# Split stores of three output tiles and another order of steps in a fused linear-attention and gated-MLP kernel

## The chip, the cores and the metric

The kernel runs on one core of a Trainium2 chip. The metric is the device time of one execution, in microseconds, measured on the chip. A core has TensorE (PE) for matmuls, VectorE (DVE), ScalarE (ACT) and GpSimd (POOL) for elementwise work, and SyncE (SP), which issues this kernel's DMA transfers between HBM and the on-chip memory SBUF. Matmuls write to PSUM.

## The reference

The kernel adds two branches and a residual. S = 2048 tokens, D = 512, H = 32 heads of 16, F = 1792. Inputs are bf16. `B_x` is not used: both branches work on `A_x`.

```python
x   = A_x
xn  = layernorm(x)
# branch A: linear attention with a "hedgehog" feature map
q, k, v = split(xn @ wqkv)                     # per head, 16 wide
phi(t)  = concat(softmax(t @ w_phi), softmax(-t @ w_phi))   # 32 features per head
kv  = phi(k)^T @ v ;  z = sum over tokens of phi(k)
A   = ((phi(q) @ kv) / (phi(q) . z + 1e-6)) @ wo
# branch B: gated MLP without a nonlinearity
B   = ((xn @ w_gate) * (xn @ w_up)) @ w_down
out = x + A + B
```

## The kernel before

The 2048 tokens are 16 tiles of 128, in four groups of four. The program is a long prologue written in place (loads, the first tiles' layer norm, the first value projections) and then a list of named steps. Each step is a small function in a dictionary `steps`, and the string `ORDER` (from line 25 on) names all of them in the order in which they are issued. The suffix `/v`, `/g` or `/a` runs an elementwise step on DVE, POOL or ACT. A second table, `SLOTS`, says which buffer of a ring each new tile takes: the PSUM banks (`s`), working tiles (`x`), feature maps (`phi`), transposed attention outputs (`oT`), output tiles (`o`) and so on. Nothing reorders the steps afterwards: each engine, SP too, runs its own instructions in the order of the list, and an instruction waits for its inputs, for its buffer to come free, and for all that is ahead of it on its engine.

The names that matter, with the line that does the work. A number behind a name is a tile or a weight block:

- `g`, `u`, `gc`, `h`: gate and up matmuls of one 128-column block of F for 512 tokens (line 333), the copy of the gate to SBUF (339 and 341) and the product (353). Tokens 0 to 1023 go this way.
- `fk`, `fq`: matmuls that fold `w_phi` into the k and q weights (455). `s`, `sc`, `a`, `xt`: layer norm of tiles 4 to 15, and the DMA transpose of the result (507).
- `vk`, `k`, `q`: projections (319). `x` and `y` behind k or q: the two exponentials on ACT (521); `r` and `i`: sums and their reciprocals on DVE (533, 538); `kp`, `qp`: the normalised features on POOL (543).
- `kv`, `kvm`: the sum of phi(k)^T v over all tiles (574) and its masked copy (579); `vc` copies the values to SBUF. `qt`: DMA transpose of phi(q) (600). `ab`: phi(q) against kv in PSUM (611); `de`, `rd`, `ot`: denominator, reciprocal, quotient (622 to 639); `oT`: DMA transpose of the quotient (645).
- `f`, `fs`, `fo`: the down projection and `wo` of one token tile (663), its sum with x (673, 676) and its store (680). `F` is the last quarter of tile 12's columns.
- `p`, `k`, `j`, `m`, `d4`: for tokens 1024 to 2047 the gate and up products are taken by a scheme with seven half-size matmul products in place of eight, for 7 pairs of blocks of F (797). It needs sums of tokens `z` (774) and of weights `up`, `t` (758), copies `k` of products (339, 341), joins `j` on DVE (812, 816) and products `m` of gate and up (819).
- `P`, `K`, `A`, `B`, `J`, `X`: the down projection of six of the last eight tiles, taken as the pairs (9, 13), (10, 14) and (11, 15), uses the same scheme. It needs sums `S` of the hidden values (894) and copies and differences of the down weights `cb`, `ct`, `wt` (874). `P2a.9` is the first part of product 2 of pair 9 (matmuls at 924), `P2w.9` the attention part of tile 9 through `wo`. Products stay in PSUM or are copied by `K` (341), `A` and `B` add to the copy (947), and `J` joins on DVE into one half, 256 columns, of an output tile `o_sb` (953). `J2` and `J3` fill the two halves of the earlier tile of the pair, `J4` (columns 0 to 255) and `J8` (256 to 511) those of the later one. `X` stores a finished tile (979).

Two rules are added by the code that walks the list. When a DVE step reads and writes only SBUF (`both_in_sbuf`: names `z`, `t`, `wt`, `cb`, `ct`, `S`, `m`, `A`, `B`, `a`, `ws` with a number), the next POOL instruction of the list waits for it. When a PSUM phase begins (`=k`, `=ab`, `=f`, `=ab2`), two banks change hands.

The walk and the store, word for word:

```python
    for word in ORDER.split():
        name, _, eng = word.partition("/")
        fn, default = steps.pop(name)
        ...
        if on_pool and turn is not None:
            tc.add_manual_dep(on_pool[0], turn.name, AFTER, reason="turns")
            turn = None
        if on_dve and both_in_sbuf.match(name):
            turn = on_dve[-1]
...
        for t in (n, m):
            steps[f"X{t}"] = (lambda t=t: nc.sync.dma_start(out=out_view(t, t + 1)[:, 0, :], in_=mine["o", t][:]), None)
```

Of the kernel before, what the change touches and what calls it, by code (L numbers as in the profile page):

```python
# [20 lines left out]
def _bcast_ap(ap_in: bass.AP, new_ap):  # L21
# [1 line left out]


ORDER = """
g2 gc2/v u0 g3 gc3/a u2 h2 g1 u1 gc1/v h1 fk2 g0 gc0/v u3 fka2/a h3 h0 fk0 fkv0/v g8 g4 fkv2/a fka0/a k0 gc8/v
s7 u8 h8 s5 s6 s4 gc4/a n1.1 ky0 k1 n0.1 n0.3 kx0 ky1 kr0 ki0 g10 g7 gc10/a sc4 a6/g k3 u4 u6 h4 gc7/a xt6 g9 g6
u10 s8 s11 a7/v n1.6 kx1 a4/a u7 gc6/a g13 xt7 n0.0 ky3 xt4 h10 u13 h6 u9 gc13/a gc9/a a5/a xt5 h7 kr1 s14 ki1
h9 n1.4 g12 gc12/v kp0/g =k k2 u12 u5 g5 h12 s10 h13 n0.5 kx3 n0.2 kx2 n1.5 ky2 s9 sc8 a9/g u14 g14 gc14/a gc5/v
h5 kp1/g a8/g xt9 g15 g20 kv0 h14 wq n0.4 u20 g18 gc15/a n1.2 n0.6 gc18/a gc20/a s13 kr3 s12 s15 kr2 u18 vk5.0  # L30
vk5.1 ky5 vc5/a h20 g16 gc16/v h18 ki3 g24 vk4.0 vk4.1 u16 ki2 kx5 n1.0 n2.3 kr5 gc24/a u15 kv1 vc4/a sc12 a13/g
kp3/g kp2/g vk6.0 g19 h16 h15 vk6.1 gc19/v kx4 ky4 n1.3 fq2 wr0 ki5 a10/v wf0 vc6/v u19 kv2 kx6 fqv2/a ky6 g21
fq0 xt10 fqv0/a g23 gc23/a fqa2/v h19 gc21/a kr6 kr4 ki4 a15/g g17 u21 u24 a12/a xt12 xt15 kv3 h24 wp0 kp5/g xt8
ki6 h21 kp4/g ws0 up00/v kp6/g u23 a14/a xt14 fqa0/a gc17/a vk7.0 vk7.1 kx7 ky7 vc7/v kr7 h23 up01/g vk9.0 kv4
g26 gc26/a kv5 vk9.1 a11/a t00/g kx9 ky9 kr9 ki7 u26 up21/a vk8.0 vk10.0 h26 vc9/v vk8.1 kx8 ky8 kr8 vk10.1 u17
h17 kp7/g t01/g up30/a vc10/a ki9 kp9/g kx10 t03/g g11 ky10 q0.0 q0.1 g25 gc25/a gc11/a vc8/v xt11 xt13 kr10
t02/v ki8 ki10 u11 u27 h11 kv6 vk12.0 g27 gc27/v h27 kv7 qx0 n2.5 kp8/g kp10/g qy0 n2.2 qr0 vk12.1 qi0 u25 h25
qp0/g qt0 ky12 kx12 up40/a kr12 vk11.0 vk11.1 ki12 vc12/a kv8 ky11 kx11 vc11/a kr11 kp12/g ki11 vk13.0 vk13.1
ky13 kx13 kr13 ki13 q1.0 g22 q1.1 kv9 u22 vk14.0 kv10 vk14.1 qy1 gc22/a qx1 h22 up20/a kp11/g vk15.0 q4.0 kp13/g
vk15.1 qr1 ky14 kx14 qi1 qp1/g vc14/a kx15 ky15 kv11 q4.1 q5.0 kr14 ki14 vc15/a vc13/a qx4 q2.0 q2.1 f1.6 qy4  # L40
f2.0 kv12 q7.0 q5.1 kr15 q3.0 ki15 qr4 qi4 kp14/g q3.1 f2.2 kv13 kv14 f1.4 kp15/g qy2 qx2 qr2 qi2 qp4/g qt1 qy3
qx3 kv15 f1.5 kvm0 p1.1 f0.0 f1.1 kvm1 =ab ab0 up11/a qx5 qp2/g qy5 up10/a qr3 de0 q7.1 f0.3 f0.2 f2.6 qy7 qx7
k1.1/a f0.5 f0.6 f0.1 p2.1 f2.1 f3.0 n2.1 n2.6 n2.0 n2.4 qi3 z0/v z1/v rd0 ot0 qp3/g z2/g ab1 p6.1 f1.3 j2.1
f1.2 f2.4 p1.0 f0.4 qt2 oT0 de1 qt3 qr5 rd1 ot1 f0.7 qr7 f0.8 f2.3 f3.2 f3.5 fs0 t10/g t11/v t13/g k2.1/a wr2
p7.1 ab2 de2 rd2 up31/a k1.0/a f3.4 f2.5 p6.0 wf2 ot2 oT1 qi5 z3/g p2.0 f1.8 ab3 k2.0/a up51/a de3 qi7 j2.0 f1.0
f3.3 k3.1/a rd3 ot3 p7.0 f1.7 f3.6 qp5/g m2.1/v qt4 oT2 f3.1 f2.7 ab4 f2.8 fs1 qp7/g de4/v fo0 oT3 qt5 k3.0/a
p4.0 fs2 p5.1 p5.0 j7.1 j7.0 rd4 ot4 wp2 t12/g d4.0/a p1.2 q6.0 q6.1 p4.1 p3.1 k1.2/a t22/g t20/g t21/g qx6 qy6
p3.0 p6.2 d4.1 qr6 f3.8 j3.0 j3.1 fo1 oT4 ab5 p1.3 up61/a k2.2/a up41/a k1.3/a p2.2 p7.2 f3.7 p1.4 p2.3 p6.3 qi6
fs3 j2.2 qt7 p5.2 de5/a k3.2/a p4.2 rd5 k1.4/a k2.3/a d4.2/a p6.4 qp6/g t23/g qt6 fo2 j2.3 ot5 j7.2 oT5 ws2
k2.4/a m7.1/g p7.3 S0.0/g S2.0/g p2.4 j2.4 ab7 p7.4 de7/a p5.3 p3.2 rd7 j3.2 k3.3/a k3.4/a p1.5 p2.5 p4.3 p4.4  # L50
j7.3 k1.5/a p6.5 ot7 k2.5/a d4.3 p1.7 ab6 j2.5 p3.3 de6/a d4.4/a j3.3 t30/g p2.7 p5.4 t31/g rd6 k1.7/a j7.4
up50/a ot6 =f m7.3/v t33/g p7.5 p2.6 p1.6 k1.6/v k3.5/a j2.7 m2.5/v p6.7 q10.0 oT6 q10.1 p4.5 p3.4 qx10 qy10
p6.6 k2.7/a f5.6 q13.0 m3.3/v j2.6 f5.3 f5.0 p5.5 cb11.1/a k2.6/a f5.2 q13.1 f5.5 qy13 j3.4 m2.3/g t32/g p7.6
k3.6/a qx13 ct2.1/a qr10 j7.5 d4.5 qi10 p7.7 p3.5 f5.7 f5.1 S0.1/g S2.1/v m7.5/v m3.1/v t40/v S0.2/v j3.5 p1.9
p5.6 p5.7 p4.6 q8.0 f5.4 qp10/g t41/g k3.7/a d4.6/a q8.1 qy8 ct1.1/a qr13 j7.6 j7.7 p1.8 f5.8 p4.7 p2.9 k1.9/v
k1.8/a qx8 p6.9 m7.7/v fs5 j2.9 m3.5/g t42/v wt1.1/v qi13 f4.5 p3.6 j3.6 qr8 wt2.1/g q14.0 k2.9/a p7.9 k3.9/a
p2.8 p3.7 f4.1 p6.8 f4.6 p5.8 q14.1 f4.7 k2.8/a p7.8 j2.8 qt10 qi8 qp13/g d4.7 t43/v q12.0 q15.0 q12.1 qx14 qy14
k3.8/a t50/v f4.8 f4.4 m2.9/v t52/g qp8/g qr14 j7.8 j3.7 t51/v q9.0 f4.2 p3.8 f4.0 t53/v p4.8 q15.1 p4.9 p1.11
f4.3 q9.1 qy12 qx12 d4.8/a j3.8 d4.9 p1.10 k1.11/a ct2.0/a qx9 p5.9 k1.10/a p6.11 p2.10 S0.3/g S2.2/g S1.2/g
m3.7/g qt13 fo3 p2.11 qr12 fs4 oT7 up60/a qi14 qp14/g j7.9 qi12 f6.1 f6.2 f6.7 k2.11/a qp12/g qt14 qt12 f6.8  # L60
t60/g qy9 j2.11 f6.0 j2.10 m7.9/v qr9 qi9 m2.7/v cb11.0/a p5.11 f7.8 p3.9 p6.10 k2.10/a qx15 f7.5 p7.11 p1.12
j3.9 S1.1/v p7.10 f6.3 f6.4 f7.1 t61/v t63/g k3.11/a ct1.0/a qy15 j7.11 k3.10/v qt8 fo4 k1.12/a f7.6 p1.13 f6.5
f6.6 f7.2 p5.10 p4.10 f7.3 f7.0 qp9/g m2.11/g S0.4/v f7.7 f7.4 qr15 j7.10 fs6 qi15 p3.10 p3.11 m7.11/v p4.11 fs7
=ab2 j3.10 j3.11 qp15/g inv d4.10/a k1.13/a p6.13 d4.11 k2.13/a t62/v wt1.0/g S0.5/g p6.12 f12.4 p2.13 ab12
p5.12 j2.13 k2.12/a de12/a cb22.0/a p7.12 k3.12/a cb21.0/a rd12 F12.5 p2.12 ot12 oT12 qt9 p7.13 f12.1 F12.3
F12.1 j2.12 k3.13/v p4.12 m3.11/g m3.9/g p5.13 d4.12/a F12.2 ab13 p4.13 j7.12 f12.0 q11.0 q11.1 p3.12 de13/a
j7.13 d4.13 rd13 fo5 ot13 qt15 m7.13/v S1.4/g S0.6/g S1.5/g S1.3/g m2.13/v f8.5 ab8 f12.8 p3.13 qy11 qx11
cb22.1/a de8/v rd8 ot8 f12.6 P1a.10 f12.5 S1.0/v F12.4 F12.6 f12.3 F12.7 f8.0 F12.0 ab9 j3.13 S1.6/g S2.4/g
S2.5/g P1b.9 fo7 oT13 j3.12 f8.2 f12.2 P1b.10 wt2.0/v f12.7 S3.0/g oT8 F12.8 K1.10/a de9/v m3.13/v f8.1 f8.7
P1a.9 P6a.10 rd9 ot9 fs12 qr11 Fs12 S2.3/v ct3.0/a f8.3 ab14 cb21.1/a K1.9/a ct3.1/a wt3.1/v P5a.10 P5b.10 P6a.9  # L70
f8.8 P6b.9 P5a.9 de14/a rd14 ot14 wt3.0/v S3.2/v Fo12 P6b.10 f8.6 P5b.9 f8.4 qi11 S2.6/v K6.9/a P7a.9 ab10 oT9
oT14 A1.9/v qp11/g A6.9/g K5.9/a K6.10/a K5.10/v de10/a rd10 fs8 fo8 B6.9/g ot10 P8w.9 P7b.9 P7a.10 P1a.11
P7b.10 P8w.10 P2w.9 P2b.9 ab15 K7.10/a K7.9/v de15/a wt4.0/v P1b.11 K1.11/a P2a.9 qt11 S3.6/v J2.9 rd15 ot15
S3.4/g A7.9/g P4w.9 P4a.10 P4w.10 S3.1/v P6a.11 P6b.11 P5a.11 P4a.9 P5b.11 wt4.1/v K5.11/a J8.9 S3.3/v fo6 P4b.9
J4.9 A7.10/v oT15 A1.10/g A1.11/g S3.5/g K6.11/a X13 oT10 P4b.10 J4.10 J8.10 P2a.10 ab11 P3w.9 P7a.11 P7b.11
P3a.9 P2b.10 P3a.11 X14 de11/a rd11 ot11 K7.11/v P8w.11 A7.11/v J8.11 P3a.10 P3b.11 A6.11/g B6.11/g A6.10/g
B6.10/g oT11 fo12 P3b.9 J3.9 P3w.10 P2a.11 P2b.11 X9 P3w.11 P3b.10 J3.10 P2w.11 J2.11 J3.11 X11 P4a.11 P2w.10
J2.10 X10 P4w.11 P4b.11 J4.11 X15
"""

SLOTS = {
    "vt": "01234123401201241342134023",
    "s": (
        "012345120345120345123451245310245132410413042305214023512405213402510153420341532015042130412543"
        "10324153045134015230342433315440132035024013410543303253401104232152204021354432014"
    ),
    "x": "01234012340120234231042042304303410324130241041230123424034013213201140214314201301420",
    "g": "012012102102010121001020102010",
    "e": "01201201201201201201201201201201",
    "su": "01201201021021021021021021021021",  # L90
    "rs": "01201201201201201201201201201201",
    "phi": "01230132103201231023103120312012",
    "T": "0101010",
    "qt": "0123450123450153",
    "den": "0101010101010101",
    "rd": "0101010101010101",
    "ot": "0101010110101011",
    "oT": "0123401230412340",
    "o": "012012021210102",
    "f": "010010010",  # L100
}


@with_exitstack
def kernel(
# [12 lines left out]
    nc = tc.nc  # L118
    P = 128
    S, D = A_x.shape[-2], A_x.shape[-1]  # L120
# [23 lines left out]
    out_view = token_views(out)  # L144
# [35 lines left out]
    for lo in (0, 2):  # L180
        nc.sync.dma_start(out=wv[:, lo:lo + 2, :],
                          in_=A_wqkv[lo * P:(lo + 2) * P, 2 * D:3 * D].rearrange("(c p) f -> p c f", p=P))
# [230 lines left out]
    steps = {}  # L413
# [435 lines left out]
    W = D // 2  # L849
# [50 lines left out]
    def pair_steps(n):  # L900
# [74 lines left out]
        join(8, m, 1, "d", lambda: kept("k3"))  # L975
        product(4, "a", a(3, FH), d("t4"), False, (m, 0))
        join(4, m, 0, "a", lambda: x(m, 0))
        for t in (n, m):
            steps[f"X{t}"] = (lambda t=t: nc.sync.dma_start(out=out_view(t, t + 1)[:, 0, :], in_=mine["o", t][:]), None)

    t0 = 1
    LAST = 12
# [93 lines left out]
```

## Time and profile before

| what | before |
|---|---|
| median of 3 runs | 214.32 us (214.11 to 214.84) |
| the profiled execution | 214.6 us |
| its span (first to last recorded event) | 212.8 us |
| PE busy | 207.8 us, 98% of the span, 1368 matmuls |
| DVE busy | 181.5 us, 85%, 333 instructions |
| ACT busy | 138.2 us, 65%, 247 instructions |
| POOL busy | 140.3 us, 66%, 133 instructions |
| granted TensorE clock | 0.999 |
| written to HBM | 2.10 MB |

The profile is of one execution. The span lies inside the time of that execution, which is 1.8 us longer. Busy times are of instructions that compute; a busy PE counts the streaming of matmuls, while weight loads (PEld) run beside them. "Waits" lists the time in which an engine stood idle by the event that released it. The "chain that ended last" is followed back from the last instruction.

### The profile page before, as it was taken

What the parts mean: (1) busy time and instruction counts of PE and PEld (TensorE: products, weight loads), DVE (VectorE), ACT (ScalarE), POOL (GpSimd) and SP (SyncE); (2) the same over time, 40 slices, a digit from 0 to 9 for tenths busy, and PEclk for the clock granted to TensorE, in tenths of its full rate; (3) what the DMA queues carried; (4) which work ended last, traced back from release to release, by engine and by line L of the source; (5) the groups of instructions that cost most, each with busy time, mean ns of one, the idle gap of its engine ahead of it and who ended that gap; (6) DMA issues with size and microseconds to landing.
All of it is one profiled execution on the core that took longest, in us unless ns stands there. A gap on an engine that the chain in (4) does not pass through costs nothing.

```text
span 212.8 us, 3868 instructions
## 1 busy us (share of the span) xinstructions
PE 207.8 (98%) x1368; PEld 109.8 (52%) x1368; DVE 181.5 (85%) x333; ACT 138.2 (65%) x247; POOL 140.3 (66%) x133
## 2 busy tenths in 40 slices
PE   7999999999999999999999999999999999999993
PEld 3554444444454455554454444444444455678982
DVE  4857998986967889889878999999999999997853
ACT  4616999977756897889943966765487457254200
POOL 3600350776678898987887986567697888927370
PEclk9999999999999999999999999999999999999999
DMA  5999996050133002021545540020405506525342
GB/s 161 260 283 385 376 288 80 12 115 0 28 78 72 0 3 49 0 52 37 101 89 88 111 99 18 11 43 6 99 0 93 84 2 138 87 42 91 74 117 74
DMA packets 47250, 19.91 MB, mean 94 GB/s; under 512 B 37504, under 2 KB 46976, under 8 KB 47104
## 3 DMA queue, kind: packets, MB, share of 16 engines
q1 hardware_dynamic: 47232, 19.69, 41.2%
q8 instruction: 10, 0.16, 0.3%
q14 instruction: 8, 0.07, 0.1%
HBM read 8.67 MB, written 2.10 MB: 51 GB/s over the span
## 4 chain that ended last, share of the span: by engine, by line
PE 91%; DMA 3%; DVE 2%; SPq 1%; issue 1%; DVEq 0%
PE fin L663 16%; PE g L333 12%; PE u L333 11%; PE sa L797 11%; PE k L319 6%; PE pv L319 6%; PE q L319 6%; PE sc L797 5%; PE da L924 4%; PE sb L797 3%; PE kv L574 2%; DMA oT<-otok 2%; PE db L924 2%; PE dd L924 2%; PE dc L924 2%; PE ab L611 2%
## 5 line engine op out<-in xcount | busy, mean ns | idle before, releaser
L533 DVE TENSOR_REDUCE sums<-e 128x64 f32<-128x1024 f32 x32 | 38.4, 1204 | 3.5 <-ACT e L521 3.3
L543 POOL TENSOR_TENSOR phiq<-e,rs 128x1024 bf16<-128x1024 f32 x16 | 31.0, 1944 | 11.4 <-ACT dK L341 4.2
L663 PE MATMUL fin<-wd,hT 128*128 128x512 bf16 (+2 forms) x154 | 37.9, 360 | 0.0
L543 POOL TENSOR_TENSOR phik<-e,rs 128x1024 bf16<-128x1024 f32 x16 | 30.9, 1940 | 7.3 <-DVE rs L538 2.8
L333 PEld LDWEIGHTS <-wgu 128*128 128x128 bf16 x240 | 22.8, 98 | 23.4 <-DMA wgu<-in_B_w_gate_dram 0.3
L333 PE MATMUL u<-xnT,wgu 128*128 128x512 bf16 (+1 forms) x120 | 27.9, 365 | 0.0
L333 PE MATMUL g<-xnT,wgu 128*128 128x512 bf16 (+1 forms) x120 | 27.8, 365 | 0.0
L353 DVE TENSOR_TENSOR hT<-u,g_sb 128x512 bf16<-128x512 f32 (+1 forms) x30 | 18.8, 637 | 5.5 <-PE u L333 5.4
L663 PEld LDWEIGHTS <-hT 128*128 128x128 bf16 (+1 forms) x154 | 14.5, 98 | 14.8
L262 POOL TENSOR_SCALAR ve<-mv 128x1 f32<-128x1 f32 (+1 forms) x7 | 2.1, 293 | 24.9 <-DVE mv L258 24.8
L538 DVE RECIPROCAL rs<-sums 128x64 f32<-128x64 f32 x32 | 17.2, 542 | 1.2
L521 ACT ACTIVATE e<-k 128x512 f32<-128x512 f32 x24 | 13.3, 598 | 6.8 <-PE k L319 6.7
L521 ACT ACTIVATE e<-q 128x512 f32<-128x512 f32 x24 | 13.5, 601 | 6.4 <-PE q L319 6.3
L797 PEld LDWEIGHTS <-T 128*128 128x128 f16 x112 | 10.6, 98 | 11.9
L797 PE MATMUL sa<-ss,T 128*128 128x512 f16 x56 | 16.2, 379 | 0.0
L339 ACT CAST g_sb<-g 128x512 bf16<-128x512 f32 (+1 forms) x21 | 11.4, 568 | 7.1 <-PE g L333 6.5
L341 ACT ACTIVATE k<-sa 128x512 f32<-128x512 f32 x19 | 11.3, 602 | 6.1 <-PE sa L797 6.1
L339 ACT COPY k<-sa 128x512 f32<-128x512 f32 x19 | 11.2, 589 | 5.8 <-PE sa L797 4.8
L698 ACT ACTIVATE junk<-wgu 128x1024 bf16<-128x1024 bf16 x14 | 14.8, 1059 | 0.0
L319 PEld LDWEIGHTS <-xnT 128*128 128x128 bf16 x96 | 9.0, 98 | 10.7 <-ACT xnT L307 1.4
L758 POOL TENSOR_TENSOR T<-wgu,T 128x512 f16<-128x512 bf16 x9 | 10.6, 1176 | 5.8 <-DVE T L758 3.9
L319 PEld LDWEIGHTS <-x 128*128 128x128 f16 x96 | 9.0, 98 | 10.1 <-DVE otok L639 0.2
(153 smaller groups left out, 480.2 us busy)
## 6 DMA issues: line engine op xcount, KB each, us to landing
out_dram<-o_sb SPq DMA_DIRECT2D x15, 128.0 KB, 2.0
wd<-in_B_w_down_dram SPq DMA_DIRECT2D x1, 1792.0 KB, 16.1
wgu<-in_B_w_gate_dram SPq DMA_DIRECT2D x2, 640.0 KB, 7.2
wgu<-in_B_w_up_dram SPq DMA_DIRECT2D x2, 640.0 KB, 8.3
xall<-in_A_x_dram SPq DMA_DIRECT2D x1, 1024.0 KB, 12.4
xall<-in_A_x_dram SPq DMA_DIRECT2D x4, 128.0 KB, 2.6
vk<-in_A_wqkv_dram SPq DMA_DIRECT2D x2, 256.0 KB, 3.7
wgu<-in_B_w_gate_dram SPq DMA_DIRECT2D x2, 256.0 KB, 4.7
```

The source lines that it names most:

```text
L319: nc.tensor.matmul(ps, lhsT=xt(n)[:, j, :], rhs=w[:, j, :], start=(j == 0), stop=(j == DC - 1))
L333: nc.tensor.matmul(ps, lhsT=w[:, c, f * P:(f + 1) * P], rhs=xnT[:, c, T * TT + lo:T * TT + hi], start=(c == 0), stop=(c == DC - 1))
L339: A.copy(out=dst, in_=src)
L353: V.tensor_tensor(out=hT(T)[:, f, lo:hi], in0=ps, in1=g_sb[:, 0:hi - lo], op=ALU.mult)
L521: A.activation(out=held[s + "e", n][:, :, sign, :], in_=held[s, n].rearrange("p (g c) -> p g c", g=NG), func=AF.Exp, scale=(nrst if sign e ...
L533: V.tensor_reduce(out=sums[:], in_=ev(), axis=AX.X, op=ALU.add)
L538: V.reciprocal(out=rs[:].rearrange("p a b -> p (a b)"), in_=held.pop((s + "s", n))[:])
L543: eng.tensor_tensor(out=phi[:].rearrange("p g (x f) -> p (g x) f", f=DH), in0=ev(), in1=held.pop((s + "i", n))[:].to_broadcast((P, 2 * H, ...
L663: nc.tensor.matmul(held["fin", n, lo], lhsT=l, rhs=r, start=len(done) == 1, stop=len(done) == FC + DC)
L698: A.activation(out=out, in_=cols, func=AF.Square, accum_out=nrm[:, g, k:k + 1])
L797: nc.tensor.matmul(mine[bankname], lhsT=ww[:, j, :], rhs=xx[:, j, :], start=start and j == 0, stop=(j == hc - 1), skip_group_check=True)
L924: nc.tensor.matmul(mine[ps][:, 0:W], lhsT=l, rhs=r, start=bool(mine.pop((ps, "new"), False)), stop=True, skip_group_check=True)
```

## The change

The later tile of each pair (13, 14 and 15) was stored by one transfer of 128 rows by 512 columns, 128 KB. Now each of its column halves is a transfer of its own, 128 by 256, 64 KB: `X13.0` needs only `J4.9`, `X13.1` only `J8.9`, and likewise for 14 and 15. The earlier tiles (9, 10 and 11) are stored whole, as before. SP issues three transfers more.

`ORDER` and `SLOTS` are replaced throughout by another list of the same steps, found by a search. Some hundred elementwise steps are on another engine than before: 11 gate copies `gc` go from ACT to DVE, and five other copies or scalings go from DVE to ACT, and products `m`, sums `S`, token sums `z`, weight sums `t` and `wt` and the `A`, `B` additions change places between DVE and POOL in both directions. DVE has 337 instructions in the list's program where it had 332, ACT 221 where it had 225, POOL 132 where it had 133. The matmuls are the same ones in another order. `=k` stands near the front of the list.

The code, and the beginning and the end of `ORDER` with the places that the prediction names:

```diff
 ORDER = """
-g2 gc2/v u0 g3 gc3/a u2 h2 g1 u1 gc1/v h1 fk2 g0 gc0/v u3 fka2/a h3 h0 fk0 fkv0/v g8 g4 fkv2/a fka0/a k0 gc8/v
...
-j7.13 d4.13 rd13 fo5 ot13 qt15 m7.13/v S1.4/g S0.6/g S1.5/g S1.3/g m2.13/v f8.5 ab8 f12.8 p3.13 qy11 qx11
-cb22.1/a de8/v rd8 ot8 f12.6 P1a.10 f12.5 S1.0/v F12.4 F12.6 f12.3 F12.7 f8.0 F12.0 ab9 j3.13 S1.6/g S2.4/g
-S2.5/g P1b.9 fo7 oT13 j3.12 f8.2 f12.2 P1b.10 wt2.0/v f12.7 S3.0/g oT8 F12.8 K1.10/a de9/v m3.13/v f8.1 f8.7
...
-J4.9 A7.10/v oT15 A1.10/g A1.11/g S3.5/g K6.11/a X13 oT10 P4b.10 J4.10 J8.10 P2a.10 ab11 P3w.9 P7a.11 P7b.11
-P3a.9 P2b.10 P3a.11 X14 de11/a rd11 ot11 K7.11/v P8w.11 A7.11/v J8.11 P3a.10 P3b.11 A6.11/g B6.11/g A6.10/g
-B6.10/g oT11 fo12 P3b.9 J3.9 P3w.10 P2a.11 P2b.11 X9 P3w.11 P3b.10 J3.10 P2w.11 J2.11 J3.11 X11 P4a.11 P2w.10
-J2.10 X10 P4w.11 P4b.11 J4.11 X15
+g0 g3 gc3/v u3 g2 gc2/a fk0 =k h3 g1 u0 fka0/a fkv0/a gc0/a h0 gc1/a g8 fk2 g4 u1 u2 fkv2/v fka2/v k2 h1 gc4/v
...
+d4.11 p3.10 fo0 ct3.0/a p2.13 p6.12 p3.11 j3.10 p5.12 fs7 =ab2 ab13 k2.12/a p7.12 p2.12 m2.11/g S2.3/g qp15/g
+j3.11 m3.11/g j2.13 de13/a p6.13 f8.0 k3.12/a rd13 ot13 t63/v cb22.0/a S0.1/v j2.12 m7.11/g S0.5/g j7.12 qp14/g
+wt3.0/v m2.13/g f12.4 f12.2 f8.4 f8.5 ab12 p5.13 f8.3 p3.12 cb22.1/a k2.13/a p7.13 k3.13/a de12/v rd12 ot12
+p4.12 f12.5 d4.12/a ab8 f12.0 j3.12 j7.13 S1.2/v oT13 fo7 qt9 oT12 de8/a rd8 ot8 S1.1/g S2.5/g S2.4/g m7.13/v
+q11.0 q11.1 ct3.1/a qx11 qy11 S1.5/g qt15 fo4 qt14 oT8 p3.13 F12.1 f12.1 j3.13 p4.13 ab9 d4.13 wt2.0/v P1a.9
+F12.4 P1b.9 P1a.10 F12.5 f12.3 cb21.0/a de9/v S0.6/v rd9 ot9 m3.13/v P1b.10 S1.6/v wt2.1/v f12.7 f8.1 F12.6
+F12.2 K1.10/a P6a.10 f12.6 cb21.1/a K1.9/a ab14 de14/a f12.8 f8.8 f8.7 wt4.0/v P6a.9 P5a.10 P6b.10 wt3.1/g
...
+de11/v J4.9 X13.0 rd11 J8.10 X14.0 ot11 P3w.10 P5a.11 P3a.10 P3a.9 P5b.11 A6.10/v B6.10/g X14.1 K1.11/a oT15
+P2b.9 P2a.9 P3b.9 P2w.9 K5.11/v J3.10 B6.9/v P6a.11 P3w.9 J3.9 A1.10/v J2.10 P6b.11 P3b.11 P3a.11 P8w.11 K6.11/a
+P7a.11 oT11 A1.11/v J2.9 P2w.11 P7b.11 P2a.11 X13.1 A6.11/g fo12 X9 B6.11/v P2b.11 X10 J2.11 P3w.11 J3.11 X11
+K7.11/a A7.11/g J8.11 X15.1 P4b.11 P4a.11 P4w.11 J4.11 X15.0
...
-        for t in (n, m):
-            steps[f"X{t}"] = (lambda t=t: nc.sync.dma_start(out=out_view(t, t + 1)[:, 0, :], in_=mine["o", t][:]), None)
+        def store(t, lo, hi):
+            nc.sync.dma_start(out=out_view(t, t + 1)[:, 0, lo:hi], in_=mine["o", t][:, lo:hi])
+
+        steps[f"X{n}"] = (lambda: store(n, 0, D), None)
+        for c in range(2):
+            steps[f"X{m}.{c}"] = (lambda c=c: store(m, c * W, (c + 1) * W), None)
```

## The prediction

> **What bounds the kernel now.** I read the busy times first, then the chain that ended last, the waits of TensorE (PE), the windows by stage, and last the timeline of the tail.
>
> The page: span, busy times, PE's 40 slices and clock, the chain's shares by engine, then two rows of DMA issues.
>
> ```profile
> span 212.8 us, 3868 instructions
> PE 207.8 (98%) x1368; PEld 109.8 (52%) x1368; DVE 181.5 (85%) x333; ACT 138.2 (65%) x247; POOL 140.3 (66%) x133
> PE   7999999999999999999999999999999999999993
> PEclk9999999999999999999999999999999999999999
> PE 91%; DMA 3%; DVE 2%; SPq 1%; issue 1%; DVEq 0%
> ...
> out_dram<-o_sb SPq DMA_DIRECT2D x15, 128.0 KB, 2.0
> oT<-otok SPq DMA_TRANSPOSE x16, 2.4
> ```
>
> PE is full from the second slice to the last but one, at full clock. It sets the time, and the other engines matter only where they make it wait. Its whole list of waits:
>
> ```profile
> PE warm L359 <- PEq L1060: 0.8, 1, 0.8
> PE pv L319 <- DMA vk<-in_A_wqkv_dram: 0.3, 1, 0.3
> PE tp L304 <- DVE xn L277: 0.2, 1, 0.2
> ```
>
> All three are in the prologue, ahead of the list of steps. The last two windows (stretch; length; busy time and instructions of PE, PEld, DVE, ACT, POOL; clock; DMA share; GB/s):
>
> ```profile
> 130.00:180.00 50.00, 50.00 (x261) 23.41 (x260) 48.19 (x84) 31.47 (x53) 36.35 (x31) 1.00 0.26 49
> 180.00:209.00 29.00, 28.95 (x278) 23.56 (x274) 24.23 (x52) 8.83 (x18) 17.54 (x20) 1.00 0.42 82
> ```
>
> VectorE (DVE) is 96% busy from 130 to 180 us: what happens to it there has little room. The timeline of the tail: last matmuls, last join, last stores:
>
> ```profile
> 208.75 0.49 PE L924 MATMUL da<-dT,hT 128*128 128x256 f16 x3
> 209.03 1.09 SPq L979 DMA_DIRECT2D out_dram<-o_sb  x2
> 209.28 0.48 DVE L953 SCALAR_TENSOR_TENSOR o_sb<-da,inv,xall 128x256 bf16<-128x256 f32 x1 [0.28 <-PE da L924]
> ```
>
> **Which time.** The profiled execution took 214.6 us: span 212.8, and 1.8 outside it. The median of the runs is 214.32, so 0.28 comes off a forecast made on the profile. About 0.3% (0.64 us) is what a measurement of this kernel can tell from no change.
>
> **PE's work: nothing.** Both lists issue the same 1368 matmuls and weight loads in the same shapes, in another order. From start to start a 512-column matmul takes 0.216 us in the timeline, 384 columns 0.162, 256 0.109, 128 0.055. Added over the list this is 197.05 us for either kernel. Before, the list's first matmul starts at 11.72 and the last ends at 209.245: 197.53. Of the 0.48 between them 0.11 is the last matmul's drain past its pitch, 0.26 is lost time that I can place, and the rest is too thinly spread to name. What I can place:
>
> ```profile
> 185.70 0.11 PEld L663 LDWEIGHTS <-oT 128*128 128x128 bf16 x2 [0.55 <-DMA oT<-otok]
> 185.70 0.60 PE L663 MATMUL fin<-wo,oT 128*128 128x512 bf16 x2
> ```
>
> PE stood 0.22 us at f8.7 (due 185.48) for the transposed tile of oT8, landed at 185.655, and 0.04 at ab8 (179.65). A new list can refund 0.26 at most; the other order of PE gives nothing more.
>
> **The tail: -0.15 us.** Before, the join J4.11 ends at 209.76, the store X15 is issued 209.79 to 210.13, and its 128 KB land at 211.52, 1.73 after the issue began; the span ends 1.28 later. After, J8.11's half has gone as X15.1, and the last store holds 64 KB. No row has that size. Nearest rows: the 32 KB store took 1.45 (0.28 less), the other 128 KB ones 1.70 to 1.90, and a 96 KB one 1.85, so size does not show cleanly. I take 1.58, midway: -0.15, bounds -0.28 and 0. X15.1 is issued ahead of it on SP at 0.33 to 0.57, but J8.11 comes three product steps (1.2 us of PE) before J4.11, so the queue is free again.
>
> **Three more stores on SP: 0 to +0.4.** X13, X14 and X15 become six; each costs SP 0.33 to 0.53 of issuing. X13.0, X14.0 and X14.1 stand ahead of the transposes oT15 and oT11, which P8w.11 and P2w.11 wait for. By rows (issue of a transpose 1.19, landing 2.4, at worst 4.2): oT15 issued near 201 lands 203.4 to 204.8, due 204.74; oT11 issued near 202.2 lands 204.6 to 206.0, due 205.61. At the median both have 1 us of room; at the slow end PE waits 0.4. I take 0, by the median row. X14.1 waits for J8.10, and oT15 and all that follows on SP wait behind it; that wait is in the 201 above.
>
> **The list: +0.2, bounds 0 and +1.6.** About 100 steps change engine: 11 gate copies go from ScalarE (ACT) to DVE and five come back, products, token sums and weight subtractions swap between DVE and GpSimd (POOL). Each count times its row (gate copy 0.48 on ACT, 0.60 on DVE; `m` product 0.33 on DVE, 1.115 on POOL; `S` sum 0.27 and 0.87) gives DVE +3.5 us of row time, ACT -1.6, POOL +0.1. Spread over 198 us this is covered by DVE's 15% of idle time, except in the stretch from 100 to 180, where it is 4 to 12%. I set every step of the new list at its row's duration behind its producers and its engine's queue, and compared with the time at which PE is due. Nothing stands PE up for certain. The room is least at these places (due time, room): first gate product of group 1 (g20, 38.54, 0.55, behind transposes xt4 and xt7); p1.4 (122.57, 0.19); p2.4 (123.43, 0.25); ab13 (172.98, 0.35); ab8 (179.21, 0.1 to 0.55); ab9 (181.95, 0.25); ab14 (186.01, 0.25); f8.8 (186.59, behind oT8, which lands 185.4 to 186.7: stall 0 to 0.15). Before had the same kind of list: oT8 0.05, g10 0.11, ab8 0.15, p6.5 0.16, and lost 0.26. So the stalls of before go (-0.26), and oT8, g20 and one of the `ab` places are what is late next. Before's loss, 0.26, is my nearest measure of what such a list loses, and I take slightly less, +0.2; zero is the lower bound, and the slow ends together (g20 0.8, oT8 0.15, oT11 0.4, kv's V copy vc13 0.3) make 1.6.
>
> **A step's duration is not fixed.** The largest risk in the list is seen here: the timeline of POOL, then of DVE.
>
> ```profile
> 158.51 3.83 POOL L543 TENSOR_TENSOR phiq<-e,rs 128x1024 bf16<-128x1024 f32 x2 [0.27 <-ACT k L341]
> ```
> ```profile
> 160.44 2.19 DVE L819 TENSOR_TENSOR hT<-u_sb,hT 128x512 f16<-128x512 bf16 x1
> 164.32 0.36 DVE L819 TENSOR_TENSOR hT<-u_sb,hT 128x512 f16<-128x512 bf16 x1
> ```
>
> The product m7.9, with both inputs in SBUF, began 0.03 us after POOL's second `phi` (160.41 to 162.34) and took 2.19 instead of 0.36: it ended 0.3 after POOL did. One lost race costs up to 1.8. DVE has 48 such steps in either list; the code makes POOL's next instruction wait for such a DVE step, but not the DVE step for a POOL instruction already running. Other rows: 1.04 for a weight subtraction of 0.42, 1.08 to 1.14 for a down-weight one of 0.68. Seven of the 48 lost time before, 4.5 us in all, and none cost PE anything.
>
> The Trainium skill ("SBUF — State Buffer", section "Who interferes with whom") says that a DVE instruction with two SBUF inputs and a GpSimd one that reads SBUF lock each other out, and "Issue order, not op shape, decides who blocks." The pair above agrees (2.19 against 0.36). By that rule the count of such steps, equal in both lists, decides nothing, and where they fall decides all; it speaks against a new list as such, and its result is the first rival.
>
> **The sum.** 214.6 - 0.26 - 0.15 + 0.2 = 214.4 profiled; less 0.28, a median of 214.1. Its own range: best -0.26 - 0.28 gives 213.8, and stalls of 0.7 in place of 0.2 give 214.6.
>
> **Rivals.** (a) Lost races stand PE up: slower. Place: ab8, ab9, ab14 between 179 and 186 us, where wt2, wt3.0 and S sums on DVE meet qp14, qp15 and S sums on POOL ahead of the steps that feed PE; or p1.4 and p2.4 at 122. Price up to 1.8 per race less the room of 0.1 to 0.55, so it decides from a loss of 0.6 on. For it: POOL's backlog against PE in the new list grows to 11.1 us near 120 (6.8 before), DVE's to 5.6 (4.7). Against: the seven lost races of before cost PE nothing. One such stall of 1.3: 214.1 + 1.2 = 215.3.
> (b) The DMA places slip: xt7 behind g20 (0.25 to 0.8), oT15 and oT11 behind the new stores (0.4). For it: the transposes' rows reach 4.2. Against: most lie at 2.4. Together 0.8 in place of 0.2: 214.7, at worst 215.2.
> (c) Nothing stalls: 214.32 - 0.26 - 0.15 = 213.9; with the full 0.28 for the tail, 213.8.
> (d) The smaller last store lands no earlier (the 96 KB row says that size is not all): 214.1 + 0.15 = 214.25.
>
> **How the numbers follow.** Forecast 0.36, (c) 0.14, (d) 0.14, (a) 0.22, (b) 0.14. Before less 0.3% is 213.68; all the gain that I can find, 0.26 + 0.28, ends at 213.8, so faster needs something that I do not see (a prologue that starts earlier): 0.08, from (c) and the forecast. Slower, above 214.96: (a) with 0.20, (b) with 0.07, and 0.07 for several small stalls: 0.34. Within 0.3%: 0.58. The range reaches from 213.7, just below full gain, to 215.8, one stall at the price of a full race (214.1 + 1.7). The likeliest case's own range is 213.8 to 214.6.
>
> **What would show it.** Right: PE's waits after the prologue below 0.4 in all; no wait at f8.7; last matmul ending between 208.9 and 209.3; the last store a 64 KB one that lands 1.45 to 1.73 after its issue; the chain still 90% PE. Wrong: a gap of PE with DVE or POOL named as releaser between 120 and 187; a DVE instruction of 1 us or more whose row is 0.3 to 0.7, right ahead of it; a wait on x or oT transposes at 38 or after 204. A prologue that differs would make the comparison itself wrong.

## The result and the profile after

The changed kernel is slower. Its median over 9 runs is 216.30 us (215.61 to 216.72), that of the kernel before in the same runs 214.63 us (214.11 to 215.63). The ratio of the times is 1.0062, 95% interval 1.0045 to 1.0078: 1.33 us longer, with 1.0 to 1.7 possible. The forecast was 214.1, within 213.7 to 215.8. The profiled execution took 215.81 us, its span is 214.1 us (212.8 before).

The page of the changed kernel: span, busy times, PE's slices and clock, the chain by engine.

```profile
span 214.1 us, 3857 instructions
...
PE 208.4 (97%) x1368; PEld 109.7 (51%) x1368; DVE 183.9 (86%) x338; ACT 137.3 (64%) x243; POOL 141.8 (66%) x132
...
PE   7999999999999999999999999999999999899993
...
PEclk9999999999999999999999999999999999999998
...
PE 11%; DVE 2%; DMA 1%; issue 0%
```

PE's work is what it was, and the clock too. What is new is one slice below 9, from 182 to 187 us, and a chain in which PE's part breaks off: followed back from the end, it leaves PE at 187.9 and goes on through a DMA transfer, that of oT8. The waits of PE (us in total, times, longest) show another one just ahead of it:

```profile
PE warm L359 <- PEq L1064: 0.8, 1, 0.8
PE ab L611 <- DMA phiqT<-phiq: 0.7, 1, 0.7
PE pv L319 <- DMA vk<-in_A_wqkv_dram: 0.3, 1, 0.3
```

The middle line is new: one step `ab` stood for a transposed phi(q). The timeline of PE around it (start, duration; in brackets the idle time ahead and what ended it):

```profile
185.91 0.49 PE L663 MATMUL fin<-wd,hT 128*128 128x384 bf16 x2
187.07 0.30 PEld L611 LDWEIGHTS <-phiqT 128*128 128x128 bf16 x8 [1.06 <-DMA phiqT<-phiq]
187.08 0.43 PE L611 MATMUL ab<-KV,phiqT 128*128 128x68 bf16 x8 [0.68 <-DMA phiqT<-phiq]
...
187.90 0.33 PEld L663 LDWEIGHTS <-oT 128*128 128x128 bf16 x3 [0.46 <-DMA oT<-otok]
...
199.31 0.33 PEld L924 LDWEIGHTS <-oT 128*128 128x128 bf16 x4 [0.32 <-DMA oT<-otok]
```

These are ab14, which waited for qt14 (landed 187.03), f8.8 for oT8 (187.86), and P2w.10 for oT10 (199.27). Measured from matmul to matmul, against the pitch of 0.162 us at 384 columns and so on, PE lost 0.84, 0.23 and 0.20 us there, and 0.08 at ab7 (122.14, behind qt7). From the first matmul of the list to the start of the last one, against the sum of the pitches, it fell behind by 1.44 us; the kernel before by 0.31, of which 0.22 at f8.7. This number, the loss of the list, is the yardstick for the experiments.

The sum: the loss grew by 1.13; the list's first matmul started 0.17 later (11.90 for 11.72; in the other profiles here with an untouched prologue it starts at 11.57 to 11.74, so this is scatter and not the change); the tail got 0.2 shorter. Together that is 1.1 us, as between the last landings (212.63 and 211.52); the timed runs say 1.33, give or take 0.35.

### The profile page after: what moved, and what is told of

Read it like the earlier page. It is cut to its first block, busy times and chain, and to the rows that moved or that the text cites. A ratio compares the mean times of both kernels' runs of the same rounds, so it can differ in the third digit from the quotient of the medians.

```text
span 214.1 us, 3857 instructions
## 1 busy us (share of the span) xinstructions
PE 208.4 (97%) x1368; PEld 109.7 (51%) x1368; DVE 183.9 (86%) x338; ACT 137.3 (64%) x243; POOL 141.8 (66%) x132
## 5 line engine op out<-in xcount | busy, mean ns | idle before, releaser
L543 POOL TENSOR_TENSOR phik<-e,rs 128x1024 bf16<-128x1024 f32 x16 | 31.4, 1963 | 14.0 <-DVE rs L538 9.3
L663 PE MATMUL fin<-wd,hT 128*128 128x512 bf16 (+2 forms) x154 | 37.4, 360 | 0.0
L341 ACT ACTIVATE k<-sa 128x512 f32<-128x512 f32 x21 | 12.5, 602 | 9.4 <-PE sa L797 8.8
L819 POOL TENSOR_TENSOR hT<-u_sb,hT 128x512 f16<-128x512 bf16 x12 | 14.5, 1214 | 5.1 <-DVE wgu L894 3.1
L341 ACT ACTIVATE wgu<-wgu,up 128x1024 bf16<-128x1024 bf16 x13 | 14.9, 1156 | 0.0
L339 ACT COPY k<-sa 128x512 f32<-128x512 f32 x18 | 10.5, 589 | 7.0 <-PE sa L797 7.0
```

The lines of the kernel that those rows point to most:

```text
L341: A.activation(out=dst, in_=src, func=AF.Identity, scale=scale)
L543: eng.tensor_tensor(out=phi[:].rearrange("p g (x f) -> p (g x) f", f=DH), in0=ev(), in1=held.pop((s + "i", n))[:].to_broadcast((P, 2 * H, ...
L663: nc.tensor.matmul(held["fin", n, lo], lhsT=l, rhs=r, start=len(done) == 1, stop=len(done) == FC + DC)
```

## The experiments

Why was qt14 late? It is issued by SP at 182.29, its input has been ready since 180.35, and a transpose of phi(q) lands 3.07 us after its issue by the median of these traces, that is at 185.4, before ab14 is due (186.24). SP's timeline of the new kernel:

```profile
179.02 1.19 SPq L645 DMA_TRANSPOSE oT<-otok  x1
180.31 1.26 SPq L600 DMA_TRANSPOSE phiqT<-phiq  x1
181.62 0.57 SPq L680 DMA_DIRECT2D out_dram<-o_sb  x1
182.29 2.47 SPq L600 DMA_TRANSPOSE phiqT<-phiq  x1
184.85 2.53 SPq L645 DMA_TRANSPOSE oT<-otok  x2
```

In order: oT12, qt15, fo4, qt14, then oT8 and oT9. The issue of qt14 alone took 2.47 us where that of qt15 took 1.26. The view of DMA traffic from 182.7 to 182.9 us shows what else ran then (queue and kind, packets, MB, share of the engines; then the transfer issued in that stretch, with its time to landing):

```profile
q1 hardware_dynamic: 147, 0.06, 108.1%
q8 instruction: 1, 0.02, 46.5%
...
phiqT<-phiq SPq DMA_TRANSPOSE x1, 4.7
```

One packet of 16 KB (0.02 MB) of kind "instruction". It took 1.49 us; the kernel's own packets are mostly 256 bytes and take some 20 ns. Right behind it single 256-byte packets took up to 1.34 us. The kernel before has such a packet at almost the same time, 182.90, in the view from 182.88 to 183.0:

```profile
q8 instruction: 1, 0.02, 65.3%
...
oT<-otok SPq DMA_TRANSPOSE x1, 3.8
```

There it met oT8, which landed 3.8 us after its issue, and that was the 0.22 lost at f8.7. Whose code is loaded can be counted. In the new kernel PE has begun 251, 465, 687, 933, 1191, 1483, 1699, 1959, 2223 and 2461 of its matmuls and weight loads when such packets come. The ninth comes at 2221 to 2251 in all ten profiles that have all records of PE, also where other work was put ahead so that its time was another: these are loads of PE's code, one for about 250 of PE's instructions.

The Trainium skill ("Runtime: NRT & Kernel Launch", section "Instruction fetch mechanics") says that each engine's code is refilled in blocks of 16 KiB, 256 instructions, which the counts bear out for PE by the mean (246, with 214 to 292 from one packet to the next); and that "The cost of crossing a 16 KiB boundary is one DMA tail-bump, mostly hidden." Here it was not hidden for the kernel's own transfers: with one such block out of their way, the 1.07 us that PE lost at ab14 and f8.8 were gone (load_to_174, below).

The page of the profile has a second kind of code packets, of 8 KB on queue 14; whose code they carry was not counted. One of them, of 0.76 us, came at 185.79, while qt14 and oT8 were both in flight. The view from 185.7 to 186.0:

```profile
q1 hardware_dynamic: 117, 0.02, 37.9%
q14 instruction: 1, 0.01, 15.8%
```

From 185.4 to 185.7 the kernel's own queue had 336 packets. So part of the 0.84 and of the 0.23 is probably this second packet's; how much was not measured. It met qt14 only because the first load had held it: at the median, 185.4, qt14 would have landed ahead of it.

Three theories, then. Theory 1: the code load holds part of the DMA engines, and transfers in flight or queued behind it land late. Theory 2: steps of DVE that lost time against GpSimd hold ot9, and with it ab14. Theory 3: the queue by itself, several transfers back to back, is slow. All runs are compared with the kernel before, on the same chip, as a ratio of times.

**qt14_first: the ready transfer goes first.**

```diff
-S1.5/g qt15 fo4 qt14 oT8 p3.13
+S1.5/g qt14 oT8 qt15 fo4 p3.13
```

(with the two `qt` buffers of `SLOTS` swapped, so that each tile keeps its own)

> The new kernel with two transfers moved on SyncE's queue alone: qt15 and fo4 go behind oT8, so that qt14 is issued as soon as its input is ready (180.35 us in the profile of the new kernel). Theory 1, the transfer queue meets a code load: the packet of 16 KB that loads PE's code at 182.78 us holds one of the 16 DMA engines for about 1.5 us, and fo4, qt14 and oT8, in flight or queued behind it, land late (qt14 187.03, oT8 187.86). Then qt14, issued at 180.4, lands near 182.3, ahead of the load; PE's wait of 0.84 us at ab14 falls to 0.1 or less, the one of 0.23 at f8.8 to 0.2 or less, and the span is about 1.0 us shorter than the new kernel's (213.1 for 214.1), ratio to the kernel before about 1.002. Theory 2, DVE's lengthened steps (lost races against GpSimd) hold ot9 and with it ab14: the wait at ab14 stays at half or more, since ot9 (186.10) does not move.

Measured: ratio 1.0003 (0.9982 to 1.0024), span 212.7, loss of the list 0.41. PE waits neither at ab14 nor at f8.8:

```profile
185.82 0.32 PEld L608 LDWEIGHTS <-phiqT 128*128 128x128 bf16 x8 [0.21 <-issue]
185.85 0.41 PE L608 MATMUL ab<-KV,phiqT 128*128 128x68 bf16 x8
186.07 0.89 PEld L660 LDWEIGHTS <-oT 128*128 128x128 bf16 x6
```

The size came out: 0.6% of the time hung on the order of four transfers on SP. Theory 2 falls as a cause: ot9 ended at 185.70 here and ab14 started without a wait. One thing did not come out. I expected qt14 to be clear of the load; issued at 179.97 and first in its queue, it still landed at 184.89, 4.92 us later, because it was under way when the load came at 182.89. It had room for that. P2w.10 now lost 0.34 to oT10, which met the next load at 195.37.

**fo4_early: one transfer out of the way.**

```diff
-S1.2/v oT13 fo7 qt9 oT12
+S1.2/v fo4 oT13 fo7 qt9 oT12
...
-S1.5/g qt15 fo4 qt14 oT8
+S1.5/g qt15 qt14 oT8
```

> The new kernel with one transfer moved: the store fo4, which stood between qt15 and qt14, goes ahead of oT13, where SyncE's queue is idle. Then qt14 is issued 0.67 us earlier, near 181.65, and is in flight when the code load of 182.8 comes. Theory 1: it is hit and lands about 4.7 us after its issue, near 186.3; PE's wait at ab14 shrinks by the 0.67 of the move alone, from 0.84 to 0.2, and the one at f8.8 from 0.23 to 0.2 or less; 0.7 us faster than the new kernel, ratio to the kernel before about 1.003. If fo4's own packets were what held qt14 (its landing 3.1 after the issue without them), qt14 lands near 184.8 and the waits are gone, ratio about 1.001.

Measured: ratio 1.0026 (1.0005 to 1.0048). qt14, issued at 181.28, was hit (4.4 us to landing) and landed at 185.67, just in time for ab14 at 185.85; then oT8's issue took 2.29 us, it landed 4.2 us after it began, and PE waited for it:

```profile
186.11 0.49 PE L660 MATMUL fin<-wo,oT 128*128 128x384 bf16 x2
...
186.90 1.04 PE L660 MATMUL fin<-wo,oT 128*128 128x512 bf16 x4 [0.31 <-DMA oT<-otok]
```

Against the pitch PE lost 0.47 us there and nothing at ab14; theory 1's forecast was 0.4 over both places. So fo4's own packets were not what held qt14. (This trace lacks 20 of its matmul records, so no loss of the list is given.)

**code_shift: the load moved, the list untouched.**

```diff
-    warm_up(7)
+    warm_up(4)
+    warm_up(24, 1)
```

> The new kernel with its list untouched: in the warm-up of the prologue, where PE waits for data anyway, three of seven 512-column matmuls give way to 24 one-column ones, 42 more instructions of PE. Theory 1: PE's code comes in packets of 16 KB, so every load after that comes earlier by about 42/256 of the distance between two loads, the one of 182.8 us near 179. qt14 keeps its place in the queue, is issued near 182.3 and lands near 185.4 in place of 187.03, oT8 lands near 186.3; the waits at ab14 and f8.8 (1.07 us together) are gone, and the span is about 1.0 us shorter than the new kernel's, ratio to the kernel before about 1.002; the load of 196.3 moves to about 194, so that oT10 may land up to 0.5 earlier. Theory 3, the queue by itself (three transfers back to back, one behind the other) makes them late: nothing changes, qt14 lands near 187.0. Theory 2 (DVE): nothing changes either.

Measured: ratio 1.0061 (1.0041 to 1.0081). Neither side's forecast. The load moved by 1.3 us only, to 181.47: PE's instructions are short there, and 42 of them take little time. It thus fell on other transfers of the same cluster:

```profile
179.51 1.19 SPq L646 DMA_TRANSPOSE oT<-otok  x1
180.80 2.12 SPq L601 DMA_TRANSPOSE phiqT<-phiq  x1
182.97 0.57 SPq L681 DMA_DIRECT2D out_dram<-o_sb  x1
183.65 1.24 SPq L601 DMA_TRANSPOSE phiqT<-phiq  x1
```

Now the issue of qt15 is the long one (2.12) and that of qt14 the normal one (1.24), and oT12, 2.42 us to landing in the new kernel, took 4.42. qt14 was issued late because of what stood ahead of it, met an 8 KB code packet at 186.22 and landed 3.73 us after its issue, and PE waited 0.70 us at ab14. At the median of 3.07 it would have landed just when ab14 was due (186.72). The lengthening moves with the load, which speaks against theory 3, but the run did not take the load off the cluster. It also showed a price elsewhere: the first load came at 13.40 in place of 18.76, amid the loading of the gate weights, and a gate product waited 0.85 us for its chunk (landed at 16.76, for 15.81 in the new kernel).

**load_to_174: the load moved off the cluster.** 132 more instructions of PE in the prologue; list and queue untouched.

```diff
-    warm_up(7)
+    warm_up(4)
+    warm_up(30, 1)
...
-        warm_up(1)
+        warm_up(40, 1)
```

> The new kernel with its list and its queue untouched and 132 more instructions of PE in the prologue (one-column warm-up matmuls in place of four 512-column ones). Read from the waits at ab14 and f8.8 and from the landings, not from the time: the prologue is about 1 us longer, and every load of PE's code moves. The load that came at the 2225th instruction of PE, 182.8 us, should now come when PE is about 66 matmuls earlier in the list, some 174 us by the old times, where SyncE's queue has been empty since 162. Theory 1 (the code load): oT12 to oT8 are hit by no load, qt14 is issued near 182.3 plus the prologue's delay and lands 3.1 after its issue (before, 4.7), and PE waits at neither ab14 nor f8.8 by more than 0.1 us. Theory 3 (the queue by itself): qt14 lands 4.7 us after its issue as before and PE waits 0.8 us at ab14.

Measured: the load came at 175.32, when SP's queue was empty. The DMA view from 175.0 to 176.0 has nothing else in it:

```profile
DMA packets 1, 0.02 MB, mean 16 GB/s; under 512 B 0, under 2 KB 0, under 8 KB 0
...
q8 instruction: 1, 0.02, 7.9%
```

And the same view where qt14 is issued, 183.4 to 183.6:

```profile
phiqT<-phiq SPq DMA_TRANSPOSE x1, 3.2
```

Same four transfers, same order, back to back, and SP's timeline of the last three:

```profile
182.77 0.57 SPq L681 DMA_DIRECT2D out_dram<-o_sb  x1
183.45 1.24 SPq L601 DMA_TRANSPOSE phiqT<-phiq  x1
184.78 1.22 SPq L646 DMA_TRANSPOSE oT<-otok  x1
```

qt14 is issued in 1.24 us and lands 3.2 us after the issue began; oT8 lands after 2.5. PE waits at neither place:

```profile
187.40 0.42 PE L612 MATMUL ab<-KV,phiqT 128*128 128x68 bf16 x8
187.62 0.89 PEld L664 LDWEIGHTS <-oT 128*128 128x128 bf16 x6
187.65 1.35 PE L664 MATMUL fin<-wo,oT 128*128 128x384 bf16 x6
```

The loss of the list fell from 1.44 to 0.31. The span stayed at 214.1, since the longer prologue starts the list 1.09 us later; the time of 215.78 is a single one. This settles it between theories 1 and 3: the queue alone costs these transfers 0.1 us and PE nothing. The 8 KB packet came at 186.98 here, when qt14 had landed. So the run shows that the waits need the load of PE's code, not that this load made all of their length.

**All transfers of ten profiles.** The same reading can be made without an edit. I took the oT transposes after 60 us in the profiles of both kernels and of all runs but fo4_early, and parted them by whether a 16 KB code packet fell between issue and landing. Without one, 123 of them: median 2.43 us to landing, 2.39 to 3.48. With one, 37 of them: median 3.76, 2.41 to 4.42. For transposes of phi(q): 3.07 (114) and 3.88 (46). Of all transfers of the list after 60 us, none that was free of a 16 KB load took more than 1.25 us over the median of its kind; 47 that met one did.

The scatter that is left goes with the 8 KB packets. Of the 123 oT and 114 phi(q) transposes free of a 16 KB load, 23 and 32 met an 8 KB one, and 17 of these 55 took over 0.5 us more than the median, up to 1.2. The other 182 met neither, and none of them took more than 0.25 over it (oT 2.39 to 2.57, phi(q) 3.03 to 3.30).

**before_shift: the kernel before with code_shift's edit.**

> The kernel before with the same change of the warm-up. Theory 1: its load of PE's code at 182.90 us, in which oT8 is in flight (issued 181.89, landed 185.66, PE waits 0.22 us at f8.7), comes near 179; oT8 lands near 184.3 and the wait is gone: 0.2 us faster, ratio 0.999. Theories 2 and 3: no change, oT8 lands near 185.7.

Measured: ratio 1.0077 (1.0044 to 1.0111), slower, not faster. Two things went otherwise than forecast. The prologue's matmuls between 4 and 8 us followed each other at twice their usual distance (0.41 for 0.21 us) though the granted clock is given as 1.00 there, and the list began at 12.57 for 11.72. With everything later, the load came at 182.85, again in a cluster; oT8 was held behind others, but PE needed it later too, and the 0.22 of f8.7 was gone. In exchange a load at 111.3 met oT2 (3.84 us), and f2.7 lost 0.48. So a load taken from one place falls on another. In every run here the warm-up matmuls start at that slow pace (0.43), and with all seven of them the kernel before is at 0.21 by 5 us. With three of them taken out the slow pace lasted until 6.4 us in code_shift, where the list still began at 11.61, and until 8.2 here. Why it lasted longer here stays open.

**split_only: the other half of the change alone.** The old list with all six half stores: X13.0 and X13.1 in X13's place, X14 likewise, X15.1 behind fo12, X15.0 last.

> The kernel before with its own list and the split stores alone: X13 and X14 as two halves at the old place, X15.1 behind fo12, X15.0 last. Expected: the last store, 64 KB, lands about 1.53 us after its issue in place of 1.73 (1.53 is what the new kernel's showed), so 0.2 us faster, ratio 0.999; the transposes oT10 and oT11 are issued 0.4 and 0.8 us later without a wait of PE. Rival: the extra issues on SyncE make PE wait at P2w.10 or P2w.11, and it is 0.2 to 0.6 us slower.

Measured: ratio 1.0005 (0.9986 to 1.0025), no difference that shows. Both the gain and the rival's price are in the trace: X15.0 landed 1.62 us after its issue, 0.11 less than X15 before, but it was issued 0.12 after its join instead of 0.03, behind X10; and oT11, pushed from 203.15 to 204.12 by the extra issues, cost PE 0.31 at P3w.11. The loss of the list is 0.70 for 0.31.

**whole_stores: the new list with the old stores.**

```diff
-de11/v J4.9 X13.0 rd11 J8.10 X14.0 ot11
+de11/v J4.9 rd11 J8.10 ot11
...
-X14.1 K1.11/a oT15
+X14 K1.11/a oT15
...
-P2a.11 X13.1 A6.11/g
+P2a.11 X13 A6.11/g
...
-J8.11 X15.1 P4b.11 P4a.11 P4w.11 J4.11 X15.0
+J8.11 P4b.11 P4a.11 P4w.11 J4.11 X15
```

> The new kernel with the stores of before: X13, X14 and X15 whole, each where its second half stood. Expected: PE's waits at ab14, f8.8 and P2w.10 stay (1.2 us together), since the three extra issues stand after them on SyncE's queue; the last store, 128 KB, lands about 1.73 us after its issue in place of 1.53, so 0.2 us slower than the new kernel, ratio to the kernel before about 1.007. Rival (the extra stores cost the time): the same as the kernel before, 1.000 to 1.002.

Measured: ratio 1.0070 (1.0049 to 1.0091). The waits stay (0.85 at ab14, 0.23 at f8.8, 0.37 at P2w.10; loss 1.52), so the slowdown is the list's and not the stores'. The issue of the last store in the new kernel, then here (KB, us to landing):

```profile
out_dram<-o_sb SPq DMA_DIRECT2D x1, 64.0 KB, 1.5
```
```profile
out_dram<-o_sb SPq DMA_DIRECT2D x1, 128.0 KB, 1.7
```

1.53 and 1.74 us in the trace, the expected 0.2, though the two ratios, 1.0062 and 1.0070, do not part it from nothing.

**qt14_first_p2w: the list mended.** qt14_first, and P2w.10 two steps later on PE, since it was the next to wait.

```diff
-P2w.10 ab11 Fo12 A7.10/v A6.9/g fo6 P1a.11 P3b.10
+ab11 Fo12 A7.10/v A6.9/g fo6 P1a.11 P2w.10 P3b.10
```

> The run qt14_first with one more move: P2w.10, which waited 0.34 us there for oT10 (in flight while the code load of 195.4 came), goes behind ab11 and P1a.11, 0.7 us later on PE. If that wait is the last loss of the list, PE loses less than 0.1 us after the prologue, and the kernel is 0.3 us faster than qt14_first, ratio to the kernel before about 0.9985: at or just below the kernel before. If another wait takes its place (P2w.11 on oT11, J2.10 late before X10), the gain is 0.1 or less.

Measured: 214.47 us against 214.70, ratio 0.9978 (0.9957 to 1.0000). PE's list of waits has one line left, in the prologue:

```profile
PE warm L356 <- PEq L1061: 0.8, 1, 0.8
```

The loss of the list is 0.10. With two small moves on top of it the changed kernel went from 0.6% slower to level with the kernel before or slightly faster.

**before_swap_split15: the kernel before, mended the same way.** oT8 ahead of oT13 on SP (with their two `oT` buffers of `SLOTS` swapped), and only X15 in halves, X15.1 behind X9.

> The kernel before with two small edits: oT8 ahead of oT13 on SyncE's queue, and only X15 stored in two halves, X15.1 behind X9. Expected: oT8 is issued near 181.6 and lands near 185.3, still hit by the code load of 182.9, but the wait of 0.22 at f8.7 falls to 0.1 or less; the last store lands 1.53 to 1.6 after its issue in place of 1.73; together 0.3 us faster, ratio 0.9985. If X10's issue stands in the way of X15.0 (as in split_only, where X15.0 was issued 0.12 late) half of the store's gain is lost.

Measured: ratio 0.9988 (0.9966 to 1.0011). In the trace both parts are as expected: oT8 was issued at 181.41 and landed at 185.16, hit again but in time, and the last store took 1.54 us; the loss of the list is 0.09, the span 212.3. A gain of about 0.4 us by the trace is at the edge of what the runs can tell. Of the two mended lists neither is shown better than the other.

## Why the prediction was wrong, point by point

- **The same PE work: right.** The sum of the pitches is equal, and the clock full. All the difference is waiting.
- **The refund of 0.26: wrong.** The wait of f8.7 for oT8 came back as 0.23 at f8.8, where I had put 0 to 0.15. I read it as a chance of the old list; it was the load at 182.9 us, which comes at nearly the same count of PE's instructions in the new list too. There it made the issue of qt14 long, so that oT8 was issued only at 184.85, and oT8 itself then met the 8 KB packet (3.00 us to landing).
- **The tail, -0.15 with bounds -0.28 and 0: right.** 1.73 us to landing became 1.53, -0.20, and whole_stores took it back.
- **Three more stores on SP, 0 to +0.4, taken as 0: right for the new list.** oT15 landed at 204.90 and oT11 at 206.20, and PE did not wait. In the old list it cost 0.31 (split_only). My upper bound did not follow from my own rows: a landing 4.2 after issues at 201 and 202.2 is 205.2 and 206.4, so that PE waits up to 0.8 and not 0.4.
- **The list, +0.2 with bounds 0 and +1.6: this is the step that failed.** The new waits are 0.84, 0.23, 0.20 and 0.08: 1.35 us, all for DMA transposes. That 1.35 lies within the bounds is luck: the 1.6 was added up from g20, oT8, oT11 and vc13, and of these only oT8 made PE wait; the sum took 0.2. What was wrong is "every step of the new list at its row's duration" for the transposes. At its row qt14 would have landed 0.9 before ab14 was due (186.24), and it took 4.74 us for 3.07. The worst place, ab14, did stand in my row of tight places, with 0.25 of room and no input named; on DVE's side 0.14 of it was there (ot9 ended at 186.10). P2w.10 was not in the row at all: at 2.4 us oT10 would have landed 1.3 before it was due, and it took 3.90.
- **The reasoning behind it.** I treated the slow landings, "at worst 4.2", as the rare end of a row and took the median. They are not scatter: with a code load in flight 3.8 is the usual value for an oT. The page had the hint in its table of queues (10 packets of kind "instruction" on queue 8, and 8 on queue 14); set beside the late landings of the trace of before (oT3, oT6, oT8, qt5 and qt11 at a 16 KB packet, oT0, qt8 and qt12 at an 8 KB one) the rule could have been seen without any run.
- **The rivals.** (a), lost races of DVE: wrong. Its steps did lengthen (the down-weight differences with x took 1.29 us), and PE did not wait for any of them. (b), the DMA places slip: the right kind, at 0.14 and 214.7 to 215.2 too unlikely and too cheap, and with oT15, oT11 and xt7, the wrong transfers. (c) had no stalls and (d) no more than the forecast, and both fall with the list; the smaller store of (d) did land earlier. The signs that I had named for being wrong were DVE or POOL as releaser and transposes at 38 or after 204; the waits of 0.2 us and more came from 187 to 199 us and were for DMA.
- **The size.** Traces give +1.13 for the loss of the list and -0.20 for the tail, +0.93 together; the runs give +1.33, from 1.0 to 1.7. The rest is within the scatter of the prologue (0.17 in this profile) and of the runs. Part of the distance between 214.1 and 216.3 is the reference: the kernel before measured 214.63 in these runs, 0.31 more than the median that I started from; less that, the new one would be 216.0.
- **What stays argued.** That the load holds one of the 16 DMA engines, and that a transfer spread over all of them waits for that one, fits the packet times; the trace names no engine for a packet, so it is not shown. How the 1.07 us at ab14 and f8.8 divide between the 16 KB and the 8 KB packet is open, and so is whose code the 8 KB packets carry.

## What to carry to other kernels

A transfer that PE needs has two durations, one when a load of code falls into it and one when none does. The places of the loads of PE's code can be counted from PE's instruction list, to within some 30 instructions here, and a transpose issued in the 3 us ahead of one needs more room: 1.3 us for an oT by the median, up to 2.0. On an in-order DMA queue put the transfer with the nearest consumer first and stores that nobody waits for behind it: four words moved were worth 0.6% here. When slack is tabled, table it for every input of a step, also for those that look early.

## What the runs showed of the hardware that was not expected

- Loads of PE's code are packets of 16 KB that took 0.9 to 1.5 us, one for about 250 matmuls and weight loads, and they lengthen transposes in flight (median of an oT 3.76 us for 2.43, of a phi(q) 3.88 for 3.07). They can also lengthen the issue of a transpose on SP (2.47 us for 1.24 at qt14), so that everything behind it in the queue slips.
- Code packets of 8 KB do the same less often: 17 of 55 transposes that met only such a one were late by 0.6 to 1.2 us.
- A load can be moved by putting instructions into PE's stream: 132 of them brought the one of 182.8 us to 175.3, 42 only to 181.5, since it goes by count and not by time.
- As the last store of a kernel, 64 KB landed 1.52 to 1.62 us after the issue (eight profiles) and 128 KB 1.73 to 1.82 (three): half the bytes save about 0.2 us.
